# Two row blocks of v for tiles 0 and 1 put ahead of the third tile's transposes, and one tile's statistics put behind another's

## The chip, the cores and the metric

The kernel runs on one core of a Trainium2 chip. The metric is the time of one execution on the device, in microseconds (us); lower is better. Times are from several executions, and one more execution was recorded by the hardware profiler; all readings of the trace come from that one. The engines are named as the profile does: PE (TensorE, matrix multiplication), PEld (its weight loads), DVE (VectorE), ACT (ScalarE), POOL (GpSimd), SP (SyncE, which issues the transfers).

## The reference

The input x has 2048 tokens of 512 elements. It is normalised (without a learned scale), and the result xn goes through two branches whose sum is added to x:

```
xn = layernorm(x)
A: q, k, v = xn @ wqkv                      (32 heads of 16)
   phi(t)  = [softmax(t @ w_phi), softmax(-(t @ w_phi))]   for q and k, per head
   o       = phi_q @ (sum over tokens of phi_k^T v) / (phi_q . (sum over tokens of phi_k) + 1e-6)
   A       = o @ wo
B: B       = ((xn @ w_gate) * (xn @ w_up)) @ w_down        (1792 hidden columns)
out = x + A + B
```

All inputs and the output are bfloat16.

## The kernel before

The tokens are cut into 16 tiles of 128 (tile n), and four tiles make a group of 512 tokens. A row block c of a weight matrix is its rows 128c to 128c + 127; a projection of one tile is four matmuls, one for each row block, that add up in one PSUM bank. The order of instructions on each engine is the order in which they are written: a manual schedule is set for all engines, and each engine works through its own queue in that order, waiting where an operand isn't there yet.

The first group of tiles is handled by a prologue, written out by hand (L364 to L396), which the change touches. For a tile n of the first four:

- `dma_x` and its neighbours (L74 to L102) issue all loads on SP's queue: x of tiles 0 and 1, the first half of wv (row blocks 0 and 1), x of tile 2, the second half of wv, the first columns of w_gate, x of tile 3, and so on. None of these lines is changed.
- `centre(n)` computes the statistics of the tile on DVE (`ln_stats`, L157 and L158), subtracts the mean (`subtract`, L177), and computes 1/sqrt(var + eps) on POOL (`scale`, L162 and L163) into column n of `rst`. Tile 0 gets its mean in another way (`centre_by_halves`: half of it on DVE, half on ACT), and its statistics are needed only for the factor in `rst`; they are computed apart, by `ln_stats(0, ...)` and `scale(0)`.
- `lt(n)` transposes the centred tile on PE in four 128x128 blocks (L236) and copies the two halves from PSUM into `xnT` on ACT (L239).
- `proj(ps, n, wv, js)` does the matmuls of v of tile n for the row blocks js (L268). Tiles 0 and 1 use the banks pv[0] and pv[1] of their own; tiles 2 and 3 one from the pool of six.
- `vcopy(n, ...)` scales v by the tile's factor in `rst` on its way to SBUF, on ACT (L360) or on DVE (L362).

Before any of this, `warm_up(7)` puts seven matmuls of constants on PE, 512 columns each (L351), while the first tile of x is on its way. The order of the matmuls of v before the change is: row block 0 of tile 0; tile 1's transposes; row blocks 1, 2 and 3 of tile 0; row blocks 0 and 1 of tile 1; tile 2's transposes; row blocks 2 and 3 of tile 1; then tile 2's four. Behind them follow the first matmuls of the gated branch (`half`, L302, names g and u), tile 3's transposes and v.

After the prologue come the two units' other halves, the folding of w_phi into the weights of k (`fold`, L255), and the long steady part, in which projections, softmax features and matmuls of the gated branch alternate on PE, and last the output part (`fin`, L332 and L335).

Of the kernel before, what the change touches and what calls it, by code (L numbers as in the profile page):

```python
# [21 lines left out]
def kernel(  # L22
# [13 lines left out]
    P = 128  # L36
# [5 lines left out]
    DC = D // P  # L42
# [21 lines left out]
    wv = wpool.tile([P, DC, D], BF16)  # L64
# [85 lines left out]
    def bank(name, dt=F32, n=TT):  # L150
        return ps_s.tile([P, n], dt, name=name, tag="s")
# [3 lines left out]
    def ln_stats(n, mv):  # L155
        stats = lnpool.tile([P, nc.vector.BN_STATS_DIM], F32, name="stats")
        nc.vector.bn_stats(out=stats[:], in_=xall[:, n, :])  # L157
        nc.vector.bn_aggr(out=mv, in_=stats[:])  # L158
# [16 lines left out]
    def subtract(n, *means):  # L175
        xns[n] = xnpool.tile([P, D], BF16, name="xn")
        nc.vector.tensor_scalar(out=xns[n][:], in0=xall[:, n, :], scalar1=means[0],  # L177
                                scalar2=means[1] if len(means) > 1 else None, op0=ALU.subtract,
                                **(dict(op1=ALU.subtract) if len(means) > 1 else {}))

    def scale(n):
        ln_rstd(mv0[:, n:n + 1, :], 1, rst[:, n:n + 1])

    def centre(n):
        ln_stats(n, mv0[:, n, :])
        subtract(n, mv0[:, n, 0:1])
        scale(n)

    def centre_by_halves(n):
        h = D // 2  # L190
        part = consts.tile([P, 2], F32)
        junk = consts.tile([P, 2, h], BF16)
        nc.vector.tensor_scalar(out=junk[:, 0, :], in0=xall[:, n, 0:h], scalar1=1.0 / D, scalar2=0.0,
                                op0=ALU.mult, op1=ALU.add, accum_out=part[:, 0:1])
        nc.scalar.activation(out=junk[:, 1, :], in_=xall[:, n, h:D], func=AF.Identity, scale=1.0 / D,
                             accum_out=part[:, 1:2])
        subtract(n, part[:, 0:1], part[:, 1:2])
# [32 lines left out]
    def lt(n, nbanks=1):  # L230
        step = DC // nbanks
        tps = []
        for lo in range(0, DC, step):
            tp = bank("tp", BF16).rearrange("p (c t) -> p c t", c=DC)
            for c in range(lo, lo + step):
                nc.tensor.transpose(out=tp[:, c, :], in_=xns[n][:, c * P:(c + 1) * P], identity=ident[:])  # L236
            tps.append(tp)
        for lo in range(0, DC, 2):
            nc.scalar.copy(out=xnT[:, lo:lo + 2, n * P:(n + 1) * P], in_=tps[lo // step][:, lo:lo + 2, :])  # L239
# [3 lines left out]
    def make_bd():  # L243
        bo, wp = BO[:], wphi[:]
        nc.vector.tensor_tensor(out=bd[:], in0=_bcast_ap(bo, [bo.ap[0], [0, DC], [E1, 8], [1, DH]]),
                                in1=_bcast_ap(wp, [wp.ap[0], [DH, DC], [0, 8], [1, DH]]), op=ALU.mult)
# [19 lines left out]
    def proj(ps, n, w, js=range(DC)):  # L266
        for j in js:
            nc.tensor.matmul(ps, lhsT=xnT[:, j, n * P:(n + 1) * P], rhs=w[:, j, :],  # L268
                             start=(j == 0), stop=(j == DC - 1))
# [29 lines left out]
    def half(w, name, T, f, lo, hi):  # L299
        ps = bank(name)[:, 0:hi - lo]  # L300
        for c in range(DC):
            nc.tensor.matmul(ps, lhsT=w[:, c, f * P:(f + 1) * P], rhs=xnT[:, c, T * TT + lo:T * TT + hi],  # L302
                             start=(c == 0), stop=(c == DC - 1))
        return ps

    def gate_copy(ps, n):
        g_sb = gpool.tile([P, TT], BF16, name="g_sb")
        nc.scalar.copy(out=g_sb[:, 0:n], in_=ps)  # L308
        return g_sb

    def hidden(T, f, ps, g_sb, lo, hi):
        if T not in hTs:
            hTs[T] = hpool.tile([P, FC, TT], BF16, name="hT", tag="h")
        nc.vector.tensor_tensor(out=hTs[T][:, f, lo:hi], in0=ps, in1=g_sb[:, 0:hi - lo], op=ALU.mult)  # L314
# [34 lines left out]
    def warm_up(k, n=TT):  # L349
        for _ in range(k):  # L350
            nc.tensor.matmul(warm[:, 0:n], lhsT=ones[:, 0:P], rhs=ones[:, 0:n], start=True, stop=True)  # L351

    warm_up(7)

    def vcopy(n, ps, eng=nc.scalar):
        dst, src = vts[n % NV][:, :, :, 0:DH], ps.rearrange("p (a b c) -> p a b c", a=8, b=4)
        if n >= GT:
            nc.scalar.copy(out=dst, in_=src)  # L358
        elif eng is nc.scalar:
            nc.scalar.activation(out=dst, in_=src, func=AF.Identity, scale=rst[:, n:n + 1])  # L360
        else:
            eng.tensor_scalar(out=dst, in0=src, scalar1=rst[:, n:n + 1], scalar2=None, op0=ALU.mult)  # L362

    with tc.tile_pool(name="ps_v", bufs=1, space=PSUM) as ps_v:  # L364
        pv = [ps_v.tile([P, D], F32, name=f"pv{n}") for n in range(2)]
        centre_by_halves(0)
        centre(1)
        ln_stats(0, mv0[:, 0, :])
        scale(0)
        lt(0, nbanks=2)  # L370
        warm_up(1)
        proj(pv[0][:], 0, wv, range(1))
        lt(1)
        proj(pv[0][:], 0, wv, range(1, DC))
        centre(2)
        proj(pv[1][:], 1, wv, range(2))
        lt(2)
        proj(pv[1][:], 1, wv, range(2, DC))
        vcopy(0, pv[0])
        vcopy(1, pv[1])  # L380
        pv2 = bank("pv")
        proj(pv2, 2, wv)
        g = [half(wg, "g", 0, f, 0, 2 * P) for f in range(2)]
        g_sb = [gate_copy(ps, 2 * P) for ps in g]
        centre(3)
        vcopy(2, pv2, nc.vector)
        lt(3)
        for f in range(2):
            hidden(0, f, half(wu, "u", 0, f, 0, 2 * P), g_sb[f], 0, 2 * P)
        pv3 = bank("pv")  # L390
        proj(pv3, 3, wv)
        vcopy(3, pv3, nc.vector)
        make_bd()
        nc.gpsimd.tensor_scalar(out=nrst[:], in0=rst[:], scalar1=-1.0, scalar2=None, op0=ALU.mult)
        nc.gpsimd.tensor_tensor(out=r2[:], in0=rst[:], in1=rst[:], op=ALU.mult)
        nc.gpsimd.tensor_tensor(out=M4[:], in0=BO[:, 0:4, :], in1=BO[:, 4:8, :], op=ALU.add)  # L396
# [138 lines left out]
```

## Time and profile before

| | us |
|---|---|
| median of 3 runs | 221.92 (221.87 to 221.98) |
| the profiled execution | 221.84 |
| its span in the trace | 220.1 |
| PE busy | 214.6 |
| DVE busy | 140.1 |
| ACT busy | 88.5 |
| POOL busy | 72.8 |

The span reaches from the first to the last instruction that the trace shows, and the profiled execution's own time is 1.74 us longer. The timeline lists the start and the length of an instruction or of a merged run of them (x4 is four of a kind), and in brackets how long the engine had been idle before it and what ended that. A matmul's length includes a drain that lies beside the next one, so the distance from start to start tells what it costs in a row. The list of transfers tells the time from a transfer's issue to its landing.

### The profile page before, as it was taken

What the parts mean: (1) busy time and instruction counts of PE and PEld (TensorE: products, weight loads), DVE (VectorE), ACT (ScalarE), POOL (GpSimd) and SP (SyncE); (2) the same over time, 40 slices, a digit from 0 to 9 for tenths busy, and PEclk for the clock granted to TensorE, in tenths of its full rate; (3) what the DMA queues carried; (4) which work ended last, traced back from release to release, by engine and by line L of the source; (5) the groups of instructions that cost most, each with busy time, mean ns of one, the idle gap of its engine ahead of it and who ended that gap; (6) DMA issues with size and microseconds to landing.
All of it is one profiled execution on the core that took longest, in us unless ns stands there. A gap on an engine that the chain in (4) does not pass through costs nothing.

```text
span 220.1 us, 3494 instructions
## 1 busy us (share of the span) xinstructions
PE 214.6 (97%) x1282; PEld 104.6 (48%) x1306; DVE 140.1 (64%) x240; ACT 88.5 (40%) x164; POOL 72.8 (33%) x64
## 2 busy tenths in 40 slices
PE   8999999999999999999999999999999999999994
PEld 3564445444444444444554444444444444454443
DVE  5667976886598767657499874197655745454321
ACT  4635587458654775464444221231332322100000
POOL 3600556363338473635135433033023033000000
PEclk9999999999999999999999999999999999999999
DMA  5999995202202241202017345214431431412401
GB/s 156 265 298 392 370 230 105 55 0 51 48 0 48 51 73 24 48 3 47 2 21 127 71 96 118 52 24 95 95 74 24 95 71 28 94 49 71 73 25 48
DMA packets 47249, 19.91 MB, mean 90 GB/s; under 512 B 37504, under 2 KB 46976, under 8 KB 47104
## 3 DMA queue, kind: packets, MB, share of 16 engines
q1 hardware_dynamic: 47232, 19.69, 37.1%
q8 instruction: 10, 0.16, 0.3%
q14 instruction: 7, 0.06, 0.1%
HBM read 8.67 MB, written 2.10 MB: 49 GB/s over the span
## 4 chain that ended last, share of the span: by engine, by line
PE 89%; DVE 3%; DMA 2%; issue 2%; ACT 2%; POOL 1%; SPq 1%; DVEq 0%; ACTq 0%
PE fin L332 22%; PE g L302 20%; PE u L302 20%; PE fin L335 6%; PE q L268 6%; PE pv L268 6%; PE k L268 5%; PE ab L477 2%; DMA wv<-in_A_wqkv_dram 2%; PE kv L416 2%; DVE sums L283 1%; SPq L75 1%; ACT e L279 1%; DVE stats L157 1%; DVE rs L285 1%
## 5 line engine op out<-in xcount | busy, mean ns | idle before, releaser
L302 PE MATMUL g<-xnT,wg 128*128 128x512 bf16 (+1 forms) x227 | 57.2, 371 | 0.4
L302 PE MATMUL u<-xnT,wu 128*128 128x512 bf16 (+1 forms) x231 | 57.5, 372 | 0.1
L314 DVE TENSOR_TENSOR hT<-u,g_sb 128x512 bf16<-128x512 f32 (+1 forms) x58 | 37.2, 648 | 25.3 <-PE u L302 14.1
L308 ACT CAST g_sb<-g 128x512 bf16<-128x512 f32 (+1 forms) x58 | 33.3, 575 | 47.9 <-PE g L302 47.6
L287 POOL TENSOR_TENSOR phiq<-e,rs 128x1024 bf16<-128x1024 f32 x16 | 30.9, 1932 | 62.9 <-DVE rs L285 54.1
L283 DVE TENSOR_REDUCE sums<-e 128x64 f32<-128x1024 f32 x32 | 38.9, 1216 | 20.1 <-ACT e L279 20.1
L332 PE MATMUL fin<-wd,hT 128*128 128x512 bf16 (+2 forms) x231 | 50.3, 366 | 0.3
L287 POOL TENSOR_TENSOR phik<-e,rs 128x1024 bf16<-128x1024 f32 x16 | 30.9, 1932 | 44.8 <-DVE rs L285 32.6
L302 PEld LDWEIGHTS <-wu 128*128 128x128 bf16 x232 | 22.6, 98 | 25.7
L332 PEld LDWEIGHTS <-hT 128*128 128x128 bf16 x238 | 22.4, 98 | 24.7
L302 PEld LDWEIGHTS <-wg 128*128 128x128 bf16 x232 | 22.0, 98 | 23.6
L268 PEld LDWEIGHTS <-xnT 128*128 128x128 bf16 x192 | 17.4, 98 | 19.0 <-ACT xnT L239 1.1
L268 PE MATMUL pv<-wv,xnT 128*128 128x512 bf16 x62 | 22.5, 387 | 0.6 <-DMA wv<-in_A_wqkv_dram 0.4
L343 DVE TENSOR_TENSOR o_sb<-fin,xall 128x512 bf16<-128x512 f32 (+2 forms) x13 | 8.5, 650 | 20.5 <-PE fin L335 19.7
L268 PE MATMUL k<-W1k,xnT 128*128 128x512 bf16 x61 | 20.7, 379 | 0.0
L285 DVE RECIPROCAL rs<-sums 128x64 f32<-128x64 f32 x32 | 17.7, 553 | 3.1
L335 PE MATMUL fin<-wo,oT 128*128 128x512 bf16 (+2 forms) x66 | 16.3, 366 | 0.1
L268 PE MATMUL q<-W1q,xnT 128*128 128x512 bf16 x60 | 16.0, 378 | 0.2
L277 ACT ACTIVATE e<-q 128x512 f32<-128x512 f32 x12 | 7.2, 597 | 22.2 <-PE q L268 22.2
L358 ACT CAST vt<-pv 128x512 bf16<-128x512 f32 x12 | 7.0, 587 | 16.9 <-PE pv L268 16.9
L487 DVE TENSOR_TENSOR otok<-ab,rden 128x512 bf16<-128x512 f32 x16 | 11.1, 691 | 0.6
L157 DVE BATCH_NORM_STATS2 stats<-xall 128x6 f32<-128x512 bf16 x16 | 10.7, 668 | 0.8 <-DMA xall<-in_A_x_dram 0.8
(60 smaller groups left out, 126.7 us busy)
## 6 DMA issues: line engine op xcount, KB each, us to landing
out_dram<-o_sb SPq DMA_DIRECT2D x15, 128.0 KB, 1.9
wd<-in_B_w_down_dram SPq DMA_DIRECT2D x1, 1792.0 KB, 15.4
wg<-in_B_w_gate_dram SPq DMA_DIRECT2D x2, 640.0 KB, 7.0
wu<-in_B_w_up_dram SPq DMA_DIRECT2D x2, 640.0 KB, 8.1
xall<-in_A_x_dram SPq DMA_DIRECT2D x1, 1024.0 KB, 12.0
xall<-in_A_x_dram SPq DMA_DIRECT2D x4, 128.0 KB, 2.5
wv<-in_A_wqkv_dram SPq DMA_DIRECT2D x2, 256.0 KB, 3.5
wg<-in_B_w_gate_dram SPq DMA_DIRECT2D x2, 256.0 KB, 4.6
```

The lines of the kernel that those rows point to most:

```text
L157: nc.vector.bn_stats(out=stats[:], in_=xall[:, n, :])
L268: nc.tensor.matmul(ps, lhsT=xnT[:, j, n * P:(n + 1) * P], rhs=w[:, j, :], start=(j == 0), stop=(j == DC - 1))
L283: nc.vector.tensor_reduce(out=sums[:], in_=ev, axis=AX.X, op=ALU.add)
L285: nc.vector.reciprocal(out=rs[:].rearrange("p a b -> p (a b)"), in_=sums[:])
L287: nc.gpsimd.tensor_tensor(out=phi[:].rearrange("p g (x f) -> p (g x) f", f=DH), in0=ev, in1=rs[:].to_broadcast((P, 2 * H, DH)), op=ALU.mult)
L302: nc.tensor.matmul(ps, lhsT=w[:, c, f * P:(f + 1) * P], rhs=xnT[:, c, T * TT + lo:T * TT + hi], start=(c == 0), stop=(c == DC - 1))
L308: nc.scalar.copy(out=g_sb[:, 0:n], in_=ps)
L314: nc.vector.tensor_tensor(out=hTs[T][:, f, lo:hi], in0=ps, in1=g_sb[:, 0:hi - lo], op=ALU.mult)
L332: nc.tensor.matmul(ps, lhsT=hTs[T][:, f, t4 * P:(t4 + 1) * P], rhs=wd[:, f, lo:lo + w], start=(f == 0), stop=False)
L335: nc.tensor.matmul(ps, lhsT=oTs[n][:, c, :], rhs=wo[:, c, lo:lo + w], start=False, stop=(c == DC - 1))
L343: nc.vector.tensor_tensor(out=o_sb[:], in0=ps, in1=xres, op=ALU.add)
L487: nc.vector.tensor_tensor(out=o_tok[:].rearrange("p (b h d) -> p b h d", b=2, d=DH), in0=abv[:, :, :, 0:DH], in1=rden[:].to_broadcast((P, ...
```

## The change

One matmul of 128 columns is added to the warm-up. `centre(2)` is moved ahead of tile 0's statistics and factor: on DVE tile 2's statistics and subtraction come before tile 0's statistics, on POOL tile 2's factor before tile 0's. On PE row blocks 0 and 1 of tiles 0 and 1 are done first, then tile 2's transposes, then row blocks 2 and 3 of tile 0 and of tile 1. On ACT v of tile 1 is copied before v of tile 0. No transfer is moved and none added. Lines further down have numbers three higher in the changed kernel.

```diff
     warm_up(7)
+    warm_up(1, P)
...
         pv = [ps_v.tile([P, D], F32, name=f"pv{n}") for n in range(2)]
+        lower, upper = range(DC // 2), range(DC // 2, DC)
         centre_by_halves(0)
         centre(1)
+        centre(2)
         ln_stats(0, mv0[:, 0, :])
         scale(0)
         lt(0, nbanks=2)
         warm_up(1)
         proj(pv[0][:], 0, wv, range(1))
         lt(1)
-        proj(pv[0][:], 0, wv, range(1, DC))
-        centre(2)
-        proj(pv[1][:], 1, wv, range(2))
+        proj(pv[0][:], 0, wv, range(1, DC // 2))
+        proj(pv[1][:], 1, wv, lower)
         lt(2)
-        proj(pv[1][:], 1, wv, range(2, DC))
+        proj(pv[0][:], 0, wv, upper)
+        proj(pv[1][:], 1, wv, upper)
+        vcopy(1, pv[1])
         vcopy(0, pv[0])
-        vcopy(1, pv[1])
         pv2 = bank("pv")
         proj(pv2, 2, wv)
```

## The prediction

> **What bounds the kernel now.** I read the page first, for who is busy.
>
> ```profile
> PE 214.6 (97%) x1282; PEld 104.6 (48%) x1306; DVE 140.1 (64%) x240; ACT 88.5 (40%) x164; POOL 72.8 (33%) x64
> PE   8999999999999999999999999999999999999994
> DMA  5999995202202241202017345214431431412401
> ```
>
> TensorE (PE) works in 97% of the span, and 38 of its 40 slices say 9. Whatever shortens the kernel has to take work or idle time from PE. All the edits lie in the first 10 us. The chain that ended last, the early part of which is copied here (start, length, what), shows what PE hangs on there: first a transfer, then PE itself.
>
> ```profile
> 2.68 4.01 DMA wv<-in_A_wqkv_dram
> 6.74 1.02 PE pv L268 x4
> 7.76 0.22 PE tp L236 x4
> 7.98 0.43 PE pv L268 x2
> 8.42 0.03 issue
> 8.45 1.04 PE pv L268 x4
> 9.49 0.87 PE g L302 x8
> ```
>
> The second half of wv (rows 2 and 3) is issued at 2.68 and lands 4.01 later, at 6.69; PE goes on at 6.74. The timeline of PE has the idle time around it.
>
> ```profile
> 4.83 0.61 PE L268 MATMUL pv<-wv,xnT 128*128 128x512 bf16 x1
> 5.24 0.63 PE L236 MATMUL tp<-ident,xn 128*128 128x128 bf16 x4
> 5.66 0.63 PE L268 MATMUL pv<-wv,xnT 128*128 128x512 bf16 x1
> 6.74 1.02 PE L268 MATMUL pv<-wv,xnT 128*128 128x512 bf16 x4 [0.44 <-DMA wv<-in_A_wqkv_dram]
> 7.60 0.39 PE L236 MATMUL tp<-ident,xn 128*128 128x128 bf16 x4
> 7.82 1.67 PE L268 MATMUL pv<-wv,xnT 128*128 128x512 bf16 x6
> 9.32 1.04 PE L302 MATMUL g<-xnT,wg 128*128 128x256 bf16 x8
> ```
>
> The durations hold a drain that overlaps the next matmul, so I count start to start. The seven warm-up matmuls follow each other every 0.43 us; from 6.74 on four take 0.86 (6.74 to 7.60), 0.215 each. So PE ran at half speed until somewhere between 5.66 and 6.74, although the granted clock says 1.00 in every stretch. At half speed the matmul started at 5.66 fills PE until 6.09. From there to 6.74 PE has nothing to do: **0.65 us**. A second gap stands at 7.82: two matmuls fill PE until 8.25, and the next, the first of tile 2, starts at 8.45, after the copy of tile 2's transposes: **0.20 us**. Behind it the listing is back to back (g at 9.32, tile 3's transposes at 10.20, u at 10.42, v of tile 3 at 11.29), and the waits of PE name nothing else in the whole span but the start (0.8 us). These 0.85 us are all that the change can win from idle time.
>
> **The change, part by part.** *Extra warm-up matmul, 128 columns.* The seventh warm-up starts at 3.34 and fills PE to 3.77; four 128-column transposes at half speed go from 3.98 to 4.38, so one such matmul costs 0.10 to 0.11 us, and ends at 3.88. The first transpose waits for the subtraction of tile 0 on VectorE (3.50 + 0.41 = 3.91) and its weights load at 3.97. So it costs nothing; without that cover it would cost its 0.11.
>
> *centre(2) earlier.* On VectorE (DVE) five instructions trade places: statistics, aggregate and subtraction of tile 2 go ahead of statistics and aggregate of tile 0. The new first one waits for tile 2 of x.
>
> ```profile
> xall<-in_A_x_dram SPq DMA_DIRECT2D x1, 128.0 KB, 2.9
> ```
>
> That is the issue at 2.17, so it lands at 5.07; DVE is free at 5.04, so the wait is about 0.06 and the start 5.10. Behind it on DVE's queue stand only these rows and tile 3's statistics, which wait for their own DMA until 7.95. From tile 1's rows (statistics 3.83, weights of its transposes loaded at 5.18) it is 1.35 from the start of the statistics to the transposes: tile 2's can go at **6.45** instead of 7.13. Tile 0's statistics then start at 5.10 + 0.94 + 0.27 = 6.31 (0.94 and 0.27: statistics to subtraction, subtraction to next, of tile 1) and are aggregated by 7.21 (+0.90, as 5.04 to 5.94). GpSimd (POOL) gets two instructions for tile 2 ahead of the two for tile 0: the factor of tile 0 comes at 7.21 + 0.10 + 0.87 = 8.18 instead of 6.91 (0.87: 6.04 to 6.91). Only vcopy(0) reads it, at about 8.65 (below), so 0.47 of cover; beyond that each delay would push the gate copies behind it on ScalarE (ACT), and tile 3's copies behind those. No DMA is issued by any moved step, so SP's queue is not passed.
>
> *Rows 0 and 1 of tile 1 ahead.* pv[1]'s first two matmuls need only the first half of wv, landed at 1.71 + 3.0 = 4.71, and ACT's first copy of tile 1's transposes. That copy starts at 5.91; tile 2's copy started 8.02 and PE followed at 8.45, so 0.43 later: **6.34**. They run at 6.34 and 6.55, tile 2's transposes 6.77 to 6.99 (0.22 as 7.60 to 7.82; their input is there since 6.45), then four matmuls of rows 2 and 3 from 6.99 to 7.85. The first needs wv's second half, there since 6.69: 0.30 of cover where before PE stood waiting for it.
>
> *Tile 2.* Its copies start 0.42 after its transposes (7.60 to 8.02), at 7.19, and the first matmul of v of tile 2 could go at 7.62. PE is busy until 7.85: the second gap is gone. Four matmuls to 8.71, where g starts. g's weights are landed (3.16 + 4.3 = 7.46).
>
> *vcopy(1) ahead of vcopy(0).* The same two instructions of 1.28 us on ACT; at about 8.10 the factor of tile 1 is long there, and the second starts some 0.6 later, after tile 0's factor at 8.18. Without the swap the pair would start at 8.18: 0.1 later. Either way ACT is through at 9.4, when the first gate copy has its g (9.32 to 9.96 before, 8.71 to 9.35 now).
>
> **Sum.** Of 0.65 + 0.20 idle, 6.09 to 6.34 = 0.25 stays: PE is 0.60 ahead at g. One term takes from it: if half speed lasts beyond 6.34, the two matmuls moved there run slow. The trace brackets the switch only by the last slow matmul's end, 6.09, and 6.74: the cost is half of what reaches beyond 6.34, 0 to 0.20 us, and over an even spread some 0.06. The row nearest to it is the slow matmul at 5.66, 0.7 away, so I take the small value and keep the end. If the switch came much earlier in other executions, tile 1's transposes would end at 5.45 and everything up to the wait for wv would move up, worth at most 0.25 (from 6.99 to wv's 6.74): a gain of 0.85.
>
> **Does it stay?** All engines behind g hang on PE; what hangs on the clock on the wall are transfers. wu of units 4 to 8 lands at 11.35 + 5.9 = 17.25, wanted at 18.90 less 0.60 = 18.30. wg of these lands at 15.5, wanted at 17.4. The folded weights' transposed load lands at 12.7, wanted at 15.1. Tiles 4 to 7 of x land at 19.9, and DVE reads them at 20.64 less 0.60 = 20.04: just hidden, and tile 4's v is only at 34.25. The later pieces of the chain (DVE sums at 42.84, GpSimd's rstd at 47.29) begin with PE's own v at 40.98, so they move along. So 0.54 us come off the end. The profiled execution took 221.84 (span 220.10 and 1.74 around it), the runs' median is 221.92: 221.92 - 0.54 = **221.38**.
>
> [...]
>
> **Rivals.** *The switch to full speed comes late.* Bound to the time and not to the work, it could fall after 7.2 for the changed kernel: all work from 6.34 on to the switch takes double. With the switch at 7.54 the loss is 1.20 / 2 = 0.60: **221.9**, no change. Against it: the profile had the switch before 6.74, the three times before lie within 0.11, and a late switch would have cost the kernel before, too. 0.08.
>
> *The gap is not filled.* pv[1]'s first matmul hangs on ACT's copy; if that came 0.4 later (or PE's order held it until wv), PE would go on at 6.74 as now, and only the second gap goes: 221.92 - 0.20 = **221.72**. For it: the copy ended the idle time of PE's weight loads three times, 1.1 us in all. Against: nothing ahead of that copy changes, except the warm-up. 0.12. That the change does not do what it says can be put here: on PE the instructions stand as written, and the rest is waiting.
>
> *Tile 2 of x lands late (slower).* Its transposes now stand in PE's queue ahead of rows 2 and 3. Landing at 5.07 they have 0.32 to spare (6.45 against 6.77); each delay beyond costs PE as much. The same 128 KB for tile 3 took 4.3 from issue: at that, it lands at 6.47, the transposes start at 7.85, 1.08 late, so 0.60 - 1.08 = +0.48: **222.4**. It turns into a loss from a landing at 5.99 on. For: the transfer engines are at 0.8 to 0.9 from 2 us on. Against: its issue and all ahead of it are untouched, and the statistics of tile 2 started at 5.86 without a wait. 0.07, other losses included.
>
> **Chances.** Forecast 0.73, its own range 221.07 (gain 0.85) to 221.53 (gain 0.39). Two tenths of a per cent, 0.44 us, is about what a measurement of this kernel can tell from no change: the line is 221.48, and the end of the forecast with a slow pair lies beyond it, 0.06. So faster 0.67, same 0.06 + 0.12 + 0.07 of the late switch = 0.25, slower 0.07 and 0.01 of a switch later still = 0.08. The range goes from 221.07 to 221.75, taking in the unfilled gap.
>
> **What would show it.** In the profile after: pv at about 6.34 and not 6.74; tile 2's transposes at about 6.8; no gap before tile 2's v; g at 8.7; the span 0.5 to 0.6 shorter with PE's busy time unchanged but for 0.1. I am wrong if PE's wait for ACT or for DVE's subtraction stands where the wait for wv stood, if start to start is still 0.43 after 6.34, or if g starts at 8.7 and the end does not move, which would mean a wait behind g that I have not seen.

## The result and the profile after

The changed kernel takes 221.18 us (median of 6 runs, 220.94 to 221.44) against 221.91 (6 runs, 221.84 to 222.23): a ratio of 0.9965, 95% interval 0.9952 to 0.9978. It is faster by some 0.7 us. Beside its own variants later it took 221.40 against 222.07, a ratio of 0.9953 (0.9934 to 0.9972).

The profiled execution is the slowest of those six, 221.44 us with a span of 219.7, against 221.84 and 220.1 before. PE's share of the page first; its busy time can't be compared with 214.6 (1307 matmul records here, 1282 there: some were missing).

```profile
PE 215.7 (98%) x1307; PEld 104.5 (48%) x1307; DVE 140.1 (64%) x240; ACT 88.7 (40%) x164; POOL 72.9 (33%) x64
```

The chain that ended last, in its early part (start, length, what):

```profile
0.83 3.25 PE warm L351 x8
...
5.43 0.24 PE tp L236 x4
5.67 0.02 issue
5.69 0.38 ACT xnT L239
6.07 0.05 issue
6.12 0.61 PE pv L268 x2
6.73 0.32 PE tp L236 x4
7.05 1.85 PE pv L268 x8
```

The transfer of wv, 4.01 us of the chain before, is gone from it. The chain now starts with PE's own warm-up and, in this part, leaves PE once, for the copy of tile 1's transposes. The timeline of PE over the same stretch:

```profile
4.98 0.45 PE L268 MATMUL pv<-wv,xnT 128*128 128x512 bf16 x1
5.27 0.39 PE L236 MATMUL tp<-ident,xn 128*128 128x128 bf16 x4
5.49 0.38 PE L268 MATMUL pv<-wv,xnT 128*128 128x512 bf16 x1
6.12 0.61 PE L268 MATMUL pv<-wv,xnT 128*128 128x512 bf16 x2 [0.25 <-ACT xnT L239]
6.65 0.40 PE L236 MATMUL tp<-ident,xn 128*128 128x128 bf16 x4
7.01 1.89 PE L268 MATMUL pv<-wv,xnT 128*128 128x512 bf16 x8
8.74 1.04 PE L302 MATMUL g<-xnT,wg 128*128 128x256 bf16 x8
9.79 0.40 PE L236 MATMUL tp<-ident,xn 128*128 128x128 bf16 x4
10.02 1.04 PE L302 MATMUL u<-xnT,wu 128*128 128x256 bf16 x8
```

Three things are to be seen. Tile 1's first two matmuls of v stand at 6.12, inside what was the wait, and from 7.01 on eight matmuls of v follow without a gap up to g at 8.74 (9.32 before). (Ahead of that PE waited 0.10 for tile 2's subtraction, from 6.55 to 6.65, and 0.14 for wv, from 6.87 to 7.01; the list doesn't mark them, since the listed lengths ahead of them, 6.35 + 0.38 and 6.83 + 0.22, run to 6.73 and 7.05.) Full speed came early: tile 1's transposes took 0.22 (5.27 to 5.49), where the kernel before needed 0.42. And a small wait is new: g's eight matmuls need 0.87, so tile 3's transposes could start at 9.61; they start at 9.79, behind tile 3's subtraction.

```profile
9.38 0.35 DVE L177 TENSOR_SCALAR xn<-xall,mv 128x512 bf16<-128x512 bf16 x1
```

So g is 0.58 earlier, u 0.40 (10.42 to 10.02), and the last instruction 0.40 (217.31 to 216.91), which is the whole difference of the two profiled executions. Nothing behind u gave anything back. This trace alone doesn't say what the gain is due to: by 5.71 PE had done what took the kernel before until 6.09, so 0.38 of the 0.58 was there ahead of the moved work, by the early switch. The transfers were later in this execution: tile 2 of x took 3.1 from its issue (2.9 before) and the second half of wv 4.3 (4.01 before), landing at about 7.0.

### The profile page after: what moved, and what is told of

It is laid out like the page before. It is cut to its first block, busy times and chain, and to the rows that moved or that the text cites. A ratio compares the mean times of both kernels' runs of the same rounds, so it can differ in the third digit from the quotient of the medians.

```text
span 219.7 us, 3521 instructions
## 1 busy us (share of the span) xinstructions
PE 215.7 (98%) x1307; PEld 104.5 (48%) x1307; DVE 140.1 (64%) x240; ACT 88.7 (40%) x164; POOL 72.9 (33%) x64
## 4 chain that ended last, share of the span: by engine, by line
PE 94%; DVE 2%; ACT 1%; POOL 1%; issue 1%; DVEq 0%; ACTq 0%
PE fin L332 22%; PE g L302 20%; PE u L302 20%; PE fin L335 6%; PE q L268 6%; PE pv L268 6%; PE k L268 6%; PE ab L480 2%; PE warm L351 2%; PE kv L419 2%; PE tp L236 1%; DVE sums L283 1%; DVE stats L157 1%; POOL rstd L163 0%; PE pq L255 0%
## 5 line engine op out<-in xcount | busy, mean ns | idle before, releaser
L332 PE MATMUL fin<-wd,hT 128*128 128x512 bf16 (+2 forms) x238 | 51.1, 366 | 0.0
L268 PE MATMUL k<-W1k,xnT 128*128 128x512 bf16 x64 | 21.8, 379 | 0.0
```

Source lines behind the costliest of these rows:

```text
L332: nc.tensor.matmul(ps, lhsT=hTs[T][:, f, t4 * P:(t4 + 1) * P], rhs=wd[:, f, lo:lo + w], start=(f == 0), stop=False)
```

## The experiments

Each kernel had five rounds beside the kernel before; ratios are to that kernel in the same rounds (medians 222.07 for the first four, 222.14 for the others). Theory 1 is the prediction's: idle time of PE is filled. Theory 2: the extra warm-up matmul brings full speed forward.

**The changed kernel again.**

> The changed kernel once more, beside its own variants. Theory 1 (idle time filled): 0.4 to 0.85 below the kernel before, and in the trace the first matmul of tile 1's v stands 0.42 to 0.45 behind the start of the first copy of its transposes. Theory 2 (the clock, brought forward by the extra warm-up matmul): start to start of the matmuls goes from 0.43 to 0.215 at about 5.0 again, as in the first trace of it (0.83 warm-up to 5.27 transposes), and not behind 6.09 as in the kernel before. Rival (the early switch was chance): the switch lies elsewhere this time.

221.40 us, ratio 0.9953 (0.9934 to 0.9972), 12 runs from 221.07 to 221.83. In this trace the copy of tile 1 starts at 6.18 and its reader at 6.60, 0.42 later, as theory 1 has it. Half speed lasted longer: tile 1's transposes went from 5.51 to 5.93. So the early switch of the first trace doesn't belong to this kernel.

**Without the extra warm-up matmul.**

```diff
     warm_up(7)
-    warm_up(1, P)
```

> The change without the extra warm-up matmul. Theory 1: the same time as the changed kernel within 0.1, since the matmul ends at 3.88 ahead of the weights at 3.97. Theory 2: PE runs at half speed to about 6.1 or beyond, the transposes of tile 1 end 0.2 later, and the time is 0.15 to 0.35 above the changed kernel.

221.29 us, 0.9951 (0.9928 to 0.9974): the same as with it, without the 0.15 to 0.35 more that theory 2 expected. PE's timeline in its trace, and three pieces of its chain:

```profile
5.61 1.28 PE L268 MATMUL pv<-wv,xnT 128*128 128x512 bf16 x3
6.72 0.39 PE L236 MATMUL tp<-ident,xn 128*128 128x128 bf16 x4
7.15 1.89 PE L268 MATMUL pv<-wv,xnT 128*128 128x512 bf16 x8
```

```profile
6.28 0.61 PE pv L268 x2
6.89 0.22 PE tp L236 x4
7.15 1.89 PE pv L268 x8
```

The list merges what the chain parts: the matmul at 5.61 ran at half speed, to 6.04; the two moved ones start at 6.28, 0.22 apart, at full speed. Tile 2's transposes, from 6.72, are through at 6.94 (0.39 long, as at full speed; tile 0's, at half speed, are 0.61), and PE then waits until 7.15 for the second half of wv, issued at 2.68 and landed 4.4 later. So half speed ended between 6.04 and 6.28, as theory 2 expects of this kernel, and yet g starts at 8.87, 0.45 earlier than in the kernel before. Of that, 0.40 is idle time: 0.24 and 0.21 are left of the 0.65 and 0.20. This is the plainest trace of theory 1.

**The extra warm-up matmul alone**, in the kernel before.

> The kernel before with nothing but the extra warm-up matmul. Theory 1: the time of the kernel before within 0.1. Theory 2: half speed ends at about 5.0, but the wait for the second half of wv (6.69) swallows it, so the time is still that of the kernel before within 0.1; the trace shows the early switch.

222.03 us, 0.9998 (0.9972 to 1.0023): no change. The early switch that theory 2 expected is not in its trace either: tile 1's transposes still take 0.42 (5.21 to 5.63). (The time alone would not decide, since theory 2 expected the same here; the time of the kernel without the extra matmul does.) Theory 2 falls.

**Statistics in the old order.**

```diff
         centre(1)
-        centre(2)
         ln_stats(0, mv0[:, 0, :])
         scale(0)
+        centre(2)
```

> The change with tile 0's statistics and factor again ahead of tile 2's. Theory 1: tile 2's subtraction ends at 7.13 as before instead of 6.4 to 6.6, its transposes start at 7.2 instead of 6.65 to 6.77, and rows 2 and 3 behind them some 0.4 to 0.5 late: the time is 0.3 to 0.5 above the changed kernel and 0.1 to 0.4 below the kernel before. Rival (the order on DVE does not matter, since the second half of wv binds anyway at 6.7 to 7.0): within 0.1 of the changed kernel.

221.64 us, 0.9969 (0.9952 to 0.9986): by the medians 0.24 above the changed kernel and 0.43 below the kernel before. The intervals of the two ratios overlap, but all its 12 runs lie above the changed kernel's median, 221.40. PE's timeline:

```profile
7.19 0.40 PE L236 MATMUL tp<-ident,xn 128*128 128x128 bf16 x4 [0.34 <-DVE xn L177]
```

The transposes wait for tile 2's subtraction, as they must if the order on DVE counts. The loss is less than the expected 0.3 to 0.5, which fits the changed kernel's second trace, where these transposes stood at 7.05, not at 6.65. Its 12 runs lie within 0.13 (221.59 to 221.72), those of the changed kernel within 0.76. A wait that DVE sets at 7.19 would cover both the late transfers and the switch to full speed; that this is why is not shown.

**The statistics' order alone**, in the kernel before (`centre(2)` ahead of tile 0's statistics, all else as it was).

> The kernel before with only tile 2's statistics and subtraction ahead of tile 0's; PE's and ScalarE's order as before. Theory 1 (the gain is PE work put into the wait for the second half of wv): no gain, since that wait still stands ahead of tile 2's transposes; within 0.1 of the kernel before. Rival (the earlier subtraction brings a gain of its own): 0.2 or more below the kernel before.

222.08 us, 0.9986 (0.9959 to 1.0013): no change that can be told. PE still goes on at 6.96, when wv's second half lands. The order on DVE is worth something only with the matmuls and transposes moved.

**Only the transposes, and only the rows.** Both start from the changed kernel; the first puts `proj(pv[1][:], 1, wv, lower)` back behind tile 0's row blocks 2 and 3, the second `lt(2)`.

> The change with only tile 2's transposes put into the wait for the second half of wv: row blocks 0 and 1 of tile 1 stand behind row blocks 2 and 3 of tile 0 again. Theory 1 (a sum of idle times): PE is idle from the end of tile 0's row block 1 to tile 2's subtraction (about 6.09 to 6.45), then ten matmuls follow at 0.215 from about 6.7 to 7.0 on, so g starts at 8.85 to 9.15 instead of 8.7 to 9.0: 0.1 to 0.2 above the changed kernel, 0.45 to 0.6 below the kernel before. Rival (the matmuls are what counts, transposes are cheap): 0.4 above the changed kernel.

> The change with only row blocks 0 and 1 of tile 1 put into the wait; tile 2's transposes stand behind row blocks 2 and 3 of tile 0. Theory 1: the wait is filled but the copy of tile 2's transposes (0.85 from transposes to the first matmul that reads them) has only two matmuls, 0.43, over it, so some 0.2 of the second gap stays: 0.15 to 0.25 above the changed kernel, 0.4 to 0.55 below the kernel before. Rival (the second gap was worth nothing): within 0.05 of the changed kernel.

221.66 us (0.9973, 0.9957 to 0.9990) and 221.69 us (0.9965, 0.9944 to 0.9987), 0.26 and 0.29 above the changed kernel of the other rounds, and 0.48 and 0.45 below the kernel before. Lines of PE's timeline, of the first and of the second:

```profile
6.50 0.40 PE L236 MATMUL tp<-ident,xn 128*128 128x128 bf16 x4 [0.63 <-DVE xn L177]
6.84 2.32 PE L268 MATMUL pv<-wv,xnT 128*128 128x512 bf16 x10
```

```profile
6.05 0.61 PE L268 MATMUL pv<-wv,xnT 128*128 128x512 bf16 x2 [0.25 <-ACT xnT L239]
7.21 0.59 PE L268 MATMUL pv<-wv,xnT 128*128 128x512 bf16 x2 [0.56 <-DMA wv<-in_A_wqkv_dram]
```

Either part alone leaves idle time: the first 0.63 until the subtraction, the second 0.56 until wv, since two matmuls are not enough to fill the wait. In the second the gap ahead of tile 2's matmuls stays, too: six of them take 1.50 (7.86 to 9.36) and need 1.29. By the medians each gives about two thirds of the gain, and they overlap, as both fill the same gap; the intervals of the ratios are wider than these differences, but all 24 runs lie above 221.40. The first lost 0.26 where 0.1 to 0.2 was expected (its rival said 0.4), the second a little more than the 0.25 expected.

**No wait for the second half of wv.** Tiles 0 and 1 use rows 0 and 1 of wv in place of rows 2 and 3, so that their v, and the output, is another.

```diff
-        proj(pv[0][:], 0, wv, upper)
-        proj(pv[1][:], 1, wv, upper)
+        for n in range(2):
+            for j in upper:
+                nc.tensor.matmul(pv[n][:], lhsT=xnT[:, j, n * P:(n + 1) * P], rhs=wv[:, j - 2, :],
+                                 start=False, stop=(j == DC - 1))
```

> The changed kernel, where tiles 0 and 1 multiply row blocks 2 and 3 with rows 0 and 1 of wv instead of rows 2 and 3: the arithmetic is the same in amount, the output is another, and the first matmul behind tile 2's transposes has no wait for the second half of wv. Theory A (that wait still binds in many executions, landing at 6.7 to 7.1 against PE at 6.85 to 7.0): 0.05 to 0.25 below the changed kernel, and narrower in spread. Theory B (tile 2's subtraction and the clock bind, the second half of wv is there): within 0.05 of the changed kernel.

221.29 us, 0.9952 (0.9930 to 0.9974): not to be told from the changed kernel, 0.9953. Its trace shows why so little comes of it:

```profile
3.97 0.40 PE L236 MATMUL tp<-ident,xn 128*128 128x128 bf16 x4
...
8.45 1.04 PE L302 MATMUL g<-xnT,wg 128*128 128x256 bf16 x8
9.55 0.40 PE L236 MATMUL tp<-ident,xn 128*128 128x128 bf16 x4
```

Full speed was there at about 4 us (the transposes of tile 0 take 0.24 to the next matmul at 4.21), g started at 8.45, and then 0.23 went to tile 3's subtraction, 9.32 to 9.55. Where one transfer no longer bound, the next did.

**Tile 3 of x earlier**, issued ahead of w_gate's first columns.

> The changed kernel with tile 3 of x issued ahead of the first columns of w_gate. In both traces of the changed kernel PE waits about 0.1 to 0.2 for tile 3's subtraction ahead of its transposes (9.61 to 9.79, 9.87 to 9.95), because g now ends earlier than x of tile 3 allows. If that binds in most executions: 0.05 to 0.2 below the changed kernel. If the later columns of w_gate (landing 8.06 to 8.2, needed at 8.7 to 9.0) take its place: as much above it.

221.41 us, 0.9953 (0.9931 to 0.9975): no change. Its subtraction now starts at 8.07 and the wait ahead of tile 3's transposes is gone, but half speed lasted to about 6.8 in the profiled execution (the two moved matmuls start at 6.25 and 6.65, the transposes at 6.94) and g started at 8.89 anyway. Both changes together (this and the one before) were not run.

**Tile 2 of x later**, issued behind the second half of wv: the price of the rival on the other side.

```diff
-        if lo == 0:
-            dma_x(2, 3)
+    dma_x(2, 3)
     dma_cols(nc.sync, wg, B_w_gate, 0, 2 * P)
```

> The changed kernel with tile 2 of x issued behind the second half of wv instead of ahead of it: the price of the rival in which tile 2 lands late. It should land at about 6.3 to 6.8 instead of 5.1 to 5.4. Theory of the prediction (0.3 to spare, then one to one): tile 2's transposes start at 7.7 to 8.1 instead of 6.65 to 7.05, and the time is 0.8 to 1.2 above the changed kernel, that is 0.1 to 0.6 above the kernel before. Rival (the earlier second half of wv and the tile's own order make up for it): within 0.2 of the changed kernel.

222.05 us, 0.9997 (0.9971 to 1.0022): the whole gain is gone, 0.65 above the changed kernel, but not the 0.8 to 1.2 expected, nor slower than before. The tile landed 3.41 from its issue at 2.69, at 6.10, earlier than the 6.3 to 6.8 assumed, and the transposes waited for its subtraction:

```profile
7.49 0.40 PE L235 MATMUL tp<-ident,xn 128*128 128x128 bf16 x4 [0.48 <-DVE xn L176]
```

7.49 is 1.36 behind the start of the tile's statistics at 6.13 (the prediction has 1.35), and 0.44 to 0.84 later than in the two traces of the changed kernel. The mechanism is there, and its price too: by the prediction's sum a landing at 6.10 puts the transposes at 7.48, 0.71 behind its 6.77, which uses up the gain of 0.60 and 0.1 more. Only the landing was misjudged: one place later in the queue, the tile was not as late as tile 3's 4.3 had made me think.

**A short warm-up**: one matmul instead of eight.

> The changed kernel with one warm-up matmul at the start instead of eight, so that PE is idle from about 1.3 to 3.9. [...] Rival (the switch is bound to the start of the program, not to the work): the same time within 0.1.

222.83 us median (221.49 to 223.06), 1.4 above the changed kernel, where the rival expected the same time within 0.1: PE's work ahead of 3.9 us counts for the time here. (The ratio of the comparison, 1.0012 with 0.9989 to 1.0036, does not separate it from the kernel before; its times are widely spread.) The profiled execution is the fastest of the twelve, and there full speed came at about 6.9, after 2.5 us of idleness up to 3.89 and some 3 us of work. That the slower ones switched later is likely and not shown: none of them was traced.

**Tile 1's transposes in two banks**, `lt(1, nbanks=2)`.

> The changed kernel with tile 1's transposes in two banks, as tile 0's are, so that the first copy can start behind two transposes instead of four. The 0.25 that PE still waits for this copy shrinks by 0.1 to 0.2 (two transposes at full or half speed). If that wait is worth its size: 0.05 to 0.2 below the changed kernel, the fastest of all. If the second half of wv and tile 2's subtraction take its place: within 0.05.

221.43 us, 0.9959 (0.9943 to 0.9975): no change. The wait for the copy is gone from its trace, and PE waits for wv instead:

```profile
7.24 1.89 PE L268 MATMUL pv<-wv,xnT 128*128 128x512 bf16 x8 [0.31 <-DMA wv<-in_A_wqkv_dram]
```

No version beats the changed kernel by what can be measured.

## Why the prediction was right, point by point

- *PE idles 0.65 for wv and 0.20 for tile 2's copies, and filling that is the gain.* Right. Each half of the filling alone gives about two thirds of it, neither the statistics' order nor the warm-up matmul alone gives any, and the first trace's chain no longer holds the transfer. That g came at 8.74 there, where 8.71 was forecast, is in part luck: the early switch brought the moved matmuls 0.22 forward (6.12 for 6.34), and waits of 0.10 for tile 2's subtraction and 0.14 for wv took that back.
- *0.42 to 0.45 from the copy to its reader, so 0.25 stays idle.* The distance is right: 0.43 and 0.42 in the two traces. The 0.25 counts start to start and holds where the matmul ahead of the wait ran at half speed, as forecast: 0.24 without the extra warm-up (6.04 to 6.28). At full speed that matmul is through sooner, and 0.41 (5.71 to 6.12) and 0.45 (6.15 to 6.60) stay in the two traces of the changed kernel. The list's [0.25 <-ACT xnT L239] of the first trace counts from the end of the listed 0.38, at 5.87, and is not this number.
- *The extra warm-up matmul costs nothing.* Right, by the kernel without it (0.9951 against 0.9953).
- *The half speed costs 0.06, and an early switch could as well bring up to 0.25.* This is the term that was mis-sized. I had one bracket, 6.09 to 6.74, from one trace. The start-to-start distances of 13 traces put the switch anywhere from 3.9 (only the rows moved) over 4.0 (no wait for wv), 5.0 to 5.3 (changed kernel, first trace), 5.5 (old statistics' order) and about 6 (changed kernel, second) to about 6.8 (tile 3 earlier), a spread of 2.9; what sets the moment no run shows. The kernel before could not profit from an early one, since wv landed at 6.7 to 7.0; the changed one can.
- *0.30 of cover at wv's second half.* Too large for many executions. The landing at 6.69 in the trace of before is the earliest of all: in the other twelve with the same order of loads it is 6.8 to 7.2. In the changed kernel's first trace PE waited for it until 7.01, without the extra warm-up until 7.15; in its second trace it was early enough. But the kernel before waits longer, too (0.55 in the trace with the statistics' order alone, 0.77 in that with the extra warm-up alone, against 0.44). In the latter, with wv there at 6.99, g starts at 9.62, 0.75 behind the 8.87 of the kernel without the extra warm-up, where wv landed at about 7.1. So filling that wait is worth more than the trace of before said: a median gain of 0.73, and 0.67 in the later rounds, instead of 0.54. How much of the surplus is the early switch's and how much the transfers' the runs do not separate.
- *Tile 2's 0.32 to spare.* Its statistics started at 5.29 and 5.43 in the two traces, not at 5.10, since its transfer took 3.1 and 3.2; in the first trace PE waited 0.10 for it.
- *Tile 3's subtraction.* The prediction did not price it. It cost 0.18 in the first trace and 0.08 in the second, and nothing that the median of the kernel with tile 3 earlier shows.
- *The two copies of v on ACT.* In the first trace tile 1's started at 8.14 and tile 0's factor was there at 8.37 (7.80 + 0.57 on POOL), so the swap hid 0.23. What it is worth by itself was not tried.
- *It stays to the end.* Right: 0.40 at u, 0.40 at the last instruction.
- *Rivals.* The gap unfilled: not seen. Late switch (after 7.2, a supposition of mine): not seen in 13 traces; the latest, at about 6.8, took 221.41, so the gain is still there. Tile 2 late: mechanism and price were shown by delaying the transfer; by itself the tile was 0.2 to 0.3 later than in the trace of before, not the 1.4 of the rival.

## What to carry to other kernels

Where an engine waits in program order for a transfer, look behind the waiting instruction for work whose operands are already there, and list what each piece of it needs: here the rows needed only an old transfer and a copy, the transposes an earlier place on another engine, and neither alone filled the gap. Once a wait is filled, the next ones stand close behind it (wv, tile 3, the copy), so taking away one of them by itself shows nothing (221.29, 221.41 and 221.43 against 221.40). In the first microseconds one trace is one draw (full speed came anywhere from 3.9 to 6.8 here): read PE's speed from start-to-start distances of single instructions (a merged x3 can hide a wait), and take more traces before pricing a tenth.

## What was not expected of the hardware

PE's switch to full speed, from 0.43 to 0.215 a matmul of 512 columns, came between 3.9 and 6.8 us in kernels whose work on PE up to 3.9 us is the same but for one short warm-up matmul, while the granted clock reads 1.00 over these microseconds in all six traces where it was read by stretch, with switches at about 4.0 (no wait for wv) and 6.8 (tile 3 earlier) among them.

The kernel before has a tail: in the later rounds 14 of its 102 executions took 223.4 to 224.3 us, the others at most 222.63. The kernels that keep an idle PE near 6 to 7 us with it (extra warm-up alone 2 of 12, statistics' order alone 1, tile 2 later 3) have it too; the changed kernel and its other variants with a full warm-up have it in none of 93, with 222.22 as the highest. The record holds a hint: the granted clock, a mean over the execution, is 0.992 in 13 of the 14 (0.998 in one) and in the three such runs of the first two variants, and 0.998 to 1.000 in all other runs of these kernels. As an estimate, 0.992 over 220 us is what 3.5 us at half the clock would make (0.008 x 220 x 2), at a cost of 1.8, where these executions lie some 1.5 above the median. So the granted clock must have been lower for a while in them; when, and what brought it about, is open, since none was traced, and two variants with 0.56 and 0.63 of idle time in their traces have no such run in 12. The three of tile 2 later (223.2 to 223.4) and the slow ones of the short warm-up (222.8 to 223.1) read 1.000, so this does not explain them.
